# Four edits at a stage boundary of a Hyena filter and maxout kernel: filter stores one iteration up, the first z tile loaded in two parts, a table loaded from GpSimd, and two PSUM halves in different banks

## The chip, the cores and the metric

The kernel runs on one core of a Trainium2 chip. The time is device microseconds (us) of one execution, and the time of a kernel is the median of its runs. All arithmetic is 32-bit float. Names of engines in the profile: PE is TensorE (matmul), PEld its weight load, DVE is VectorE, ACT is ScalarE, POOL is GpSimd, SP is SyncE, which here only issues DMAs. A DMA issued by SP or ACT appears on the queue q1 or q10 (hardware_dynamic), one issued by POOL on q0 (software_dynamic).

## The reference

Two blocks in sequence. The first is a long convolution by FFT along the sequence, the second a feed-forward layer with a maximum over three branches.

```python
# x, v: (4, 12544, 128); pos_emb: (12544, 64); w1: (64, 64); w2: (64, 128)
h_filt = (np.maximum(pos_emb @ w1, 0.0) @ w2) * np.exp(-0.01 * np.arange(S))[:, None]
u = x * v
y = irfft(rfft(u, n=2*S, axis=1) * rfft(h_filt, n=2*S, axis=0)[None], n=2*S, axis=1)[:, :S]
a = (x * y).reshape(4 * 12544, 128)
# moe_w1, moe_w2, moe_w3: (128, 768); moe_w_out: (768, 128)
out = np.maximum(np.maximum(a @ moe_w1, a @ moe_w2), a @ moe_w3) @ moe_w_out
```

## The kernel before

**The transform.** The sequence of 12544 is seen as 98 blocks of 128. The FFT is done as matrix products with tables: a first stage over the block index (`u_first`, or `quad` in the prologue, 90 frequencies k1 held in two halves of 64 partitions), a second stage with a table per k1 (`g_second`), the product with the filter's spectrum (`g_re`, `g_im`), the inverse second stage (`g_third`), which leaves its result z in a DRAM tensor `zd[b]`, and the inverse first stage (`t_load`, `t_sums`, `t_last`), which reads z back by tiles of the sequence. A group g holds two frequencies; there are NK = 45 groups, and `zd[0]` has 90 rows, two for each group.

**The prologue loop.** For batch 0 the second, product and third stages run in `for s in range(NK + 3)`. In one iteration s the loop does for group s the filter's second stage (`s_second`) and the signal's (`g_second`), for group s-1 the filter's last matmul and the copy of its spectrum into the tile `ht` (`s_filter`, L1007 and L1012), for group s-2 the store of `ht` to DRAM (`s_store`, two DMAs issued by POOL, L1018), the product (L549, L553, L554) and the unfolding into `ab` (L561), and for group s-3 the third stage (L156 into `ps`), its copy `zs` (L573) and the store of `zs` to `zd[0]` (L574, issued by SP). The tile `ht` has two buffers. At s = 45 two groups, 43 and 44, are handled in one iteration: for each, in turn, `s_store`, `g_re` and `g_im`, and then both unfolds. For group 43 the addition in `g_im` (L554) is done on POOL, for all other groups on DVE.

**Work woven in.** Near the end of that loop the first units of batch 1 are begun: `unit(0)` at s = 45 and `unit(1)` after the loop. A unit is two halves; each half is 16 matmuls (L413) into one PSUM place from `banks_of`, a copy `high` by ACT (L422), and an addition and a subtraction on DVE into `spec` (L424). The six places of `banks_of` are taken in order: two for unit 0, two for unit 1, and two for the transposes of units 4 and 5 (`u_turn`, L366 and L373). The places for unit 1 are the two halves of one tile `both` of two banks. Between these lies `folding`, six times a transpose (L969), a copy (L971) and a product (`pl`), whose sum is copied to `lin` (L1085).

**The boundary.** After `pro.close()` the pools of the main stage are opened over the same memory. SP then issues the loads of the table `f4p` and of `sign` (L1092, L1094), and the two-DMA loads of z for tile 0 and tile 1 (`t_load`, L672, c = 0 and 1, 45 partitions each, each row 2 KB), with the loads of `xT` between them (L688). DVE makes the sums of tile 0 (L703, `even` and `zt`), PE runs `u_first(2)`, then `t_last` of tile 0 (the `f4p` matmuls, then L724 on DVE into `gt`), then `u_first(3)`, and then the loop of the main stage begins, whose matmuls are `up` (into `hps`) and `down` (into `ops`).

**Order.** Each engine has one queue and runs it in the order of the program text; the kernel does not let a scheduler reorder it. Semaphores are set for every dependence between tiles, also when two places of one tile don't overlap. The DMAs of SP take turns over eight semaphores, so a DMA waits for the one issued eight before it; those of POOL take turns over eight others.

## Time and profile before

| | |
|---|---|
| time, median of 3 runs | 2288.81 us (2286.15 to 2288.98) |
| the profiled execution | 2287.31 us, span 2285.5 us |
| PE | 2258.4 us busy, 99% of the span |
| PEld | 1381.6 us, 60% |
| DVE | 1558.0 us, 68% |
| ACT | 1173.6 us, 51% |
| POOL | 871.6 us, 38% |
| granted TensorE clock, mean | 0.997 |

The page shows the busy time of each engine, the chain of work that ended last, and the groups of instructions by source line. All edits of this change lie between about 280 and 320 us of the span, so the views used below are cut to that stretch: the timeline by engine (start, length, engine, line, operation, output and inputs, and in brackets the idle time before it and what ended it), the busy time by windows (with the granted clock PEclk), and the DMA view. Line numbers are those of the kernel before. Idle brackets name the releaser that came last.

### The profile page before, as it was taken

The numbers are of one execution on the slowest core, as the hardware profiler recorded it, in microseconds if no ns is written. First come the engines' busy times: TensorE is split into PE (matmuls) and PEld (weight loads), VectorE is DVE, ScalarE is ACT, GpSimd is POOL, SyncE is SP. The second block draws the span as 40 slices with busy tenths as digits, with TensorE's granted clock in tenths as the row PEclk, the third lists the DMA queues.
The fourth block names the chain that finished last, engine by engine and source line by source line (L and its number), as shares of the span: only waits on it lengthen the run. The fifth ranks groups of instructions, "written<-read, shape, count | busy, mean of one in ns | idle before, by whom it ended". The sixth has DMA issues, their size and how long they took to land.

```text
span 2285.5 us, 68501 instructions
## 1 busy us (share of the span) xinstructions
PE 2258.4 (99%) x27855; PEld 1381.6 (60%) x27855; DVE 1558.0 (68%) x2853; ACT 1173.6 (51%) x2124; POOL 871.6 (38%) x1088
## 2 busy tenths in 40 slices
PE   8999989999999999999999999999999999999998
PEld 7988866655555556655555556655555546666665
DVE  5588956667788757657878756667878854544443
ACT  2688844456666534456666534456666622222222
POOL 2044424323332333423333334413333326666666
PEclk9999999999999999999999999999999999999999
DMA  7778979799989779879999789879999832222221
GB/s 188 182 233 271 302 169 179 147 216 241 237 220 241 190 169 177 162 182 254 238 232 240 207 162 188 155 183 246 233 239 237 204 86 56 56 67 65 62 56 22
DMA packets 473270, 411.03 MB, mean 180 GB/s; under 512 B 327866, under 2 KB 374427, under 8 KB 472955
## 3 DMA queue, kind: packets, MB, share of 16 engines
q1 hardware_dynamic: 445954, 329.48, 63.8%
q0 software_dynamic: 26288, 75.47, 11.1%
q8 instruction: 219, 3.59, 0.7%
q10 hardware_dynamic: 712, 1.70, 0.3%
q14 instruction: 97, 0.79, 0.1%
HBM read 262.84 MB, written 84.67 MB: 152 GB/s over the span
## 4 chain that ended last, share of the span: by engine, by line
PE 96%; DMA 2%; DVE 1%; issue 1%; ACT 0%; SPq 0%; POOL 0%; POOLq 0%; DVEq 0%; ACTq 0%
PE hps L156 44%; PE ops L156 19%; PE ops L797 6%; PE cps L413 5%; PE cps L156 4%; PE ps L156 3%; PE cps L467 3%; PE ps L165 3%; PE cps L477 3%; PE sps L1007 2%; PE gps L989 2%; PE last L156 1%; DMA hd<-ht 1%; PE pst L366 1%; PE pm L328 1%
## 5 line engine op out<-in xcount | busy, mean ns | idle before, releaser
L156 PE MATMUL hps<-gt,w_sb 128*64 128x392 f32 x6144 | 1150.4, 494 | 0.0
L734 ACT ACTIVATE hid<-hps 128x392 f32<-128x392 f32 x768 | 383.7, 500 | 697.6 <-PE hps L156 680.8
L156 PEld LDWEIGHTS hps<-gt,w_sb 128*64 128x64 f32 x6144 | 432.6, 137 | 419.6 <-issue 384.0
L737 DVE TENSOR_TENSOR hid<-hid,hps 128x392 f32<-128x392 f32 x768 | 427.8, 557 | 332.4 <-PE hps L156 322.2
L156 PE MATMUL ops<-hid,wo_sb 128*64 128x392 f32 x2304 | 480.5, 492 | 0.0
L519 POOL TENSOR_TENSOR cb<-cb,xs 128x512 f32<-128x512 f32 x135 | 173.6, 1286 | 463.4 <-DVE xs L516 346.1
L156 PEld LDWEIGHTS ops<-hid,wo_sb 128*64 128x64 f32 x2304 | 172.8, 137 | 206.4 <-issue 197.8
L424 DVE TENSOR_TENSOR spec<-cps,high 128x360 f32<-128x360 f32 x188 | 141.0, 790 | 127.8 <-ACT high L422 127.0
L492 DVE TENSOR_TENSOR cb<-cps,eo 128x512 f32<-128x512 f32 (+1 forms) x288 | 175.1, 649 | 73.9 <-ACT eo L489 73.9
L752 POOL DMA_DIRECT2D out_dram<-ot x96 | 75.1, 783 | 345.5 <-ACT ot L750 298.0
L507 ACT ACTIVATE xs<-cb 32x512 f32<-32x512 f32 x270 | 169.5, 628 | 20.4 <-DVE cb L492 11.5
L422 ACT COPY high<-cps 128x360 f32<-128x360 f32 x94 | 75.0, 798 | 182.5 <-PE cps L413 149.1
L508 ACT COPY xs<-cb 32x512 f32<-32x512 f32 x270 | 166.3, 616 | 3.2
L413 PEld LDWEIGHTS cps<-f1q,uT 98*64 98x64 f32 x3008 | 131.9, 138 | 29.8 <-issue 23.8
L523 DVE TENSOR_TENSOR xs<-cb 128x256 f32<-128x256 f32 x270 | 140.8, 566 | 9.1 <-POOL cb L519 8.9
L413 PE MATMUL cps<-f1q,uT 98*64 98x90 f32 x3008 | 136.3, 242 | 3.2 <-DVE uT L397 1.5
L382 POOL COPY planes<-ut 128x784 uint16<-128x784 uint16 x90 | 76.4, 849 | 153.5 <-DVE ut L361 153.5
L500 POOL DMA_DIRECT2D zd<-cb x135 | 92.5, 685 | 64.5 <-DVE cb L492 56.9
L156 PEld LDWEIGHTS cps<-f4p,even 90*64 90x64 f32 x1568 | 90.8, 138 | 34.8 <-issue 32.8
L156 PE MATMUL cps<-f4p,zt 90*64 90x49 f32 x1568 | 97.4, 222 | 0.1
L821 POOL DMA_DIRECT2D out_dram<-o x128 | 77.4, 610 | 49.6 <-DVE o L814 47.9
L156 PE MATMUL cps<-f4p,even 90*64 90x49 f32 x1568 | 96.1, 220 | 0.0
(135 smaller groups left out, 3140.6 us busy)
## 6 DMA issues: line engine op xcount, KB each, us to landing
ht<-hd SPq DMA_DIRECT2D x264, 256.0 KB, 6.9
wt<-wq_const SPq DMA_DIRECT2D x144, 256.0 KB, 6.3
zd<-cb POOLq DMA_DIRECT2D x135, 256.0 KB, 6.1
zt<-zd SPq DMA_DIRECT2D x384, 90.0 KB, 3.1
sq<-spec SPq DMA_DIRECT2D x264, 128.0 KB, 7.0
ut<-in_xr_dram SPq DMA_DIRECT2D x128, 196.0 KB, 3.9
ut<-in_vr_dram SPq DMA_DIRECT2D x128, 196.0 KB, 4.1
xT<-in_x_dram SPq DMA_DIRECT2D x256, 98.0 KB, 3.3
```

The source lines that it names most:

```text
L156: nc.tensor.matmul(out[64 * h:64 * h + 64], lhsT[:, 64 * h:64 * h + 64], rhs, start=start, stop=stop, skip_group_check=True)
L413: nc.tensor.matmul(ps[64 * c:64 * c + 64, 256 * i + h * N1:256 * i + (h + 1) * N1], t[:, 2 * ((at + i) % 8) + h].rearrange("n r t -> n (r ...
L424: nc.vector.tensor_tensor(out=spec[:, :, a, at:at + n], in0=v[:, 1], in1=high, op=op)
L492: nc.vector.tensor_tensor(out=cb[:, a, lo:hi], in0=ps[:, lo:hi], in1=eo[:, lo:hi], op=op)
L500: nc.gpsimd.dma_start(zd[b][2 * z:2 * z + 2].rearrange("k c t a f -> (k c t) a f"), zss.pop(z))
L507: nc.scalar.mul(xs[at:at + 32], xt[at + 32:at + 64], -1.0)
L508: nc.scalar.copy(xs[at + 32:at + 64], xt[at:at + 32])
L519: nc.gpsimd.tensor_tensor(out=xts[g], in0=xts[g], in1=xs[:], op=ALU.add)
L523: nc.vector.tensor_tensor(out=ab[:, q], in0=y[:, 0], in1=y[:, 1], op=(ALU.subtract, ALU.add)[q])
L734: nc.scalar.activation(h[:], pa[:, 0:N], Relu)
L737: nc.vector.tensor_tensor(out=h[:], in0=h[:], in1=pb[:, 0:N], op=ALU.max)
L797: nc.tensor.matmul(ps[64 * c:64 * c + 64, 0:H2], w, rhs[:, H2 * c:H2 * c + H2], start=start, stop=True, skip_group_check=True)
```

## The change

Four edits, and no arithmetic is added or taken away.

1. `s_store` leaves the loop over `ready`. It now stands before that loop, and is called for groups 41 and 42 at s = 43, for 43 at s = 44, and for 44 at s = 45; all earlier groups keep their iteration.
2. `t_load` of batch 0, tile 0 loads groups 0 to 42 with its first two DMAs (43 partitions each) and groups 43 and 44 with two more (2 partitions each). All other tiles keep their two DMAs of 45 partitions.
3. The loads of `f4p` and `sign` are issued by POOL instead of SP.
4. `banks_of` gives unit 1 a place in the tile `h` and a place in a tile `g`, instead of the two halves of one tile `h`.

```diff
+    def load_rows(zt, i, c, lo, hi):
+        nc.sync.dma_start(
+            zt[NK * c + lo:NK * c + hi],
+            zd[0].rearrange("(g a) c t f -> g a c t f", a=2)[
+                lo:hi, :, c, 2 * i:2 * i + 2, :].rearrange("g a t f -> g a (t f)"))
+
     def t_load(b, i):
         zt = hp.tile([N1, 2, 512], FP32, tag="zt", name="zt", bufs=2)
         for c in range(2):
             if b == 0:
-                nc.sync.dma_start(
-                    zt[NK * c:NK * c + NK],
-                    zd[b].rearrange("(g a) c t f -> g a c t f", a=2)[
-                        :, :, c, 2 * i:2 * i + 2, :].rearrange("g a t f -> g a (t f)"))
+                load_rows(zt, i, c, 0, NK if i else NK - 2)
                 continue
...
+        if b == i == 0:
+            for c in range(2):
+                load_rows(zt, i, c, NK - 2, NK)
...
     def banks_of():
-        for _ in range(2):
-            yield gps.tile([P, 512], FP32, tag="g", name="ps1")[:]
-        both = sps.tile([P, 1024], FP32, tag="h", name="ps1")
-        for h in range(2):
-            yield both[:, 512 * h:512 * h + 512]
-        for pool, tag in ((cps, "cv"), (gps, "g")):
-            yield pool.tile([P, 512], FP32, tag=tag, name="pst")
+        for pool, tag, n in ((gps, "g", 1), (gps, "g", 1), (sps, "h", 2), (gps, "g", 1),
+                             (cps, "cv", 1), (gps, "g", 1)):
+            yield pool.tile([P, 512 * n], FP32, tag=tag, name="ps1")[:, 0:512]
...
         ready = [g for g in {NK: (s - 2, s - 1)}.get(s, (s - 2,)) if 0 <= g and s <= NK]
+        for g in {NK - 2: (s - 2, s - 1), NK - 1: (s - 1,), NK: (s - 1,)}.get(s, (s - 2,)):
+            if 0 <= g and s <= NK:
+                s_store(g)
         for g in ready:
-            s_store(g)
             g_re(g)
             g_im(g, g == NK - 2)
...
-    nc.sync.dma_start(f4p[:], f4p_d)
+    nc.gpsimd.dma_start(f4p[:], f4p_d)
     sign_t = hp.tile([N1, 1], FP32, name="sign", bufs=1)
-    nc.sync.dma_start(sign_t[:], sign_d)
+    nc.gpsimd.dma_start(sign_t[:], sign_d)
```

## The prediction

> **What bounds the kernel.** I read the page's busy table first, then its chain of waits, then timelines of one engine at a time around the edits.

> ```profile
> PE 2258.4 (99%) x27855; PEld 1381.6 (60%) x27855; DVE 1558.0 (68%) x2853; ACT 1173.6 (51%) x2124; POOL 871.6 (38%) x1088
> PE 96%; DMA 2%; DVE 1%; issue 1%; ACT 0%; SPq 0%; POOL 0%; POOLq 0%; DVEq 0%; ACTq 0%
> ```

> PE bounds the whole. So an edit is worth what it does to PE's idle gaps, and whatever delays PE at the boundary delays the end by as much. PE's timeline there:

> ```profile
> 289.63 1.41 PE L413 MATMUL ps<-f1q,uT 98*64 98x90 f32 x32
> 294.16 1.97 PE L156 MATMUL ps<-ab,wt 128*64 128x128 f32 x16 [3.12 <-DVE ab L561]
> ...
> 299.22 1.41 PE L413 MATMUL ps<-f1q,uT 98*64 98x90 f32 x16
> 301.97 0.84 PE L413 MATMUL ps<-f1q,uT 98*64 98x90 f32 x16 [1.34 <-DVE spec L424]
> ...
> 307.02 1.46 PE L413 MATMUL cps<-f1q,uT 98*64 98x90 f32 x32 [0.36 <-ACT lin L1085]
> ...
> 311.06 2.61 PE L413 MATMUL cps<-f1q,uT 98*64 98x90 f32 x32 [1.38 <-DVE spec L424]
> ```

> Three gaps: 3.12 us before the third stage of group 43, 1.34 us between the halves of unit 1, 1.38 us before `u_first(3)`. The windows show a second price: the granted clock (the number after POOL's) falls to half after the first and third.

> ```profile
> 294.00:294.50 0.50, 0.34 (x4) 0.30 (x6) 0.50 (x3) 0.00 (x0) 0.00 (x0) 0.60 0.76 260
> 300.50:301.00 0.50, 0.13 (x2) 0.00 (x0) 0.00 (x0) 0.28 (x1) 0.00 (x0) 0.57 0.00 0
> 311.00:311.50 0.50, 0.44 (x7) 0.47 (x9) 0.39 (x1) 0.00 (x0) 0.50 (x1) 0.67 0.36 61
> ```

> The POOL, SP and DVE timelines show what feeds these gaps:

> ```profile
> 289.03 1.27 POOL L554 TENSOR_TENSOR xt<-xt,xs 128x512 f32<-128x512 f32 x1
> 292.01 1.09 POOL L1018 DMA_DIRECT2D hd<-ht  x2 [1.71 <-ACT ht L1012]
> ...
> 300.60 0.46 SPq L1092 DMA_DIRECT2D f4p<-f4p_const  x1
> 301.11 0.37 SPq L1094 DMA_DIRECT2D sign<-sign_const  x1
> 302.39 1.89 SPq L672 DMA_DIRECT2D zt<-zd  x2
> ...
> 307.20 0.69 DVE L703 TENSOR_TENSOR even<-zt 90x512 f32<-90x512 f32 x1 [3.20 <-DMA zt<-zd]
> ```

> The two loads of z for tile 0 are issued at 302.39 and 303.43, when the last `zd` store (issued 300.13, 2.18 us to landing) is in, and DVE starts on the tile at 307.20. The DMA view of 304.2 to 305.3 us, where the first of them moves:

> ```profile
> DMA packets 108, 0.19 MB, mean 173 GB/s; under 512 B 15, under 2 KB 15, under 8 KB 108
> q1 hardware_dynamic: 108, 0.19, 63.3%
> ```

> Its 90 packets of 2 KB (one per row) pass in about 1 us, at 63% of 16 DMA engines. A packet's median time in the trace is 84 ns, so one engine alone would move 24 GB/s.

> [...] the store of 128 partitions shows 16 increments within 0.15 us, the load of `zt` (90 rows into 45 partitions[...]) one lone increment at 303.79 and 15 between 305.27 and 306.27; `f4p` (90) likewise 1 and 15. [...] The changes here, at 294.10, 300.93, 311.17 and 314.58 (transition times in the trace), fit a grid of 3.41 us.

> **Part 1, the stores.** Store 42 comes after store 41 on POOL with nothing between them before and after, store 43 likewise. The one swap is at group 43: its addition (L554, 1.27 us) stood ahead of store 44 and now stands behind it. Store 44 waits for the `ht` copy and ends at 293.10, so the addition ends at 294.4 instead of 290.3. L561 on DVE needs it and started at 293.69: 0.7 us late, with unfold 44, `u_mul` and unit 0's `spec` queued behind it. PE's 294.16 becomes 294.9, and the copies `zs` and last `zd` store (300.13) follow: **+0.7**. Bounds: 0 if other slack absorbs it, +1.3 for the whole addition.

> **Part 2, the banks.** The 1.34 us wait exists because both halves are one tile. With two, the second half follows at once; its place was last read by unit 0 at 296.6. **-1.3** (bounds -1.7 with full clock a little earlier, and -0.7 if ACT's copies then hold `folding`). Parts 1 and 2: -0.6 on PE, so `u_first(2)` starts near 306.4.

> **Part 3, `f4p` and `sign`.** SP loses 0.46 + 0.37 us of issue, which the wait for the last store hid: 0. On POOL they queue behind the addition, at 294.4, and are needed after 307; landing took 2.0 us. The idle POOL (17.6 us before its next work at 310.72) hides them; uncovered they would cost those 2 us.

> **Part 4, the split load.** SP gains two issues. The 43-row loads no longer need the last store's landing and are issued about 301.3 and 302.3 (300.60 plus 0.7, by 0.98 each). [...] **each runs on one engine, the same for both**. First packet 1.76 us after issue, as before (302.39 to 304.15): 303.06. Then 172 packets of 84 ns, 14.45 us: 317.5. The 2-row loads (4 rows[...]) queue behind on that engine. Increments trailed the last packet by 0.1 to 1.1 us; with 0.5, landed at 318.0, DVE at 318.1: **+10.9** against 307.20. What waits: `even`, `zt`, then on the same queue the `spec` of `u_first(2)`, and on PE the `f4p` matmuls with everything behind them. `spec` ends at 318.1 + 1.38 + 1.44 = 320.9. PE will have idled for ten us, so `f4p` runs at half clock: from 319.55, 2 x 1.03 us, to 321.6, when `u_first(3)` starts: **+10.5** against 311.06. The half clock then lasts to between 322.6 and 326.0; before it lasted 3.4 us past that point. At half price that is -1.2 to +0.5, I take -0.3. The `xT` shares on that engine (64 packets of about 26 ns, 1.7 us) end by 319.7, before `gt` needs them. Tile 1's loads reuse the semaphores of the 43-row loads, so they, and tile 2's and `ut` behind them on SP, are late by the same ten us; PE uses tile 1 at 323.72 in a stretch where POOL was done by 313.3, so there is slack.

> **Sum.** +10.5 - 0.3 = +10.2 (Parts 1 to 3 vanish under the longer wait except for the 0.7 us in the issue time). The profiled execution: 2287.31 + 10.2 = 2297.5. It lies 1.5 us under the median of three, which becomes 2288.81 + 10.2 = **2299.0**. PE-bound work follows, so nothing gives it back.

> **Rivals.** (A, forecast) one engine, 2299.0, own range 2297 to 2303: packets of 100 ns instead of 84 (the mean in the loaded stretch 301.5 to 310 was 119) add 2.8. (B) The 86 rows count alone, so two engines: 7.2 us of packets, landed 310.8, `u_first(3)` near 313.9: +2.9, 2291.7. [...] (C) **Not slower**: the generator spreads 43 rows over many engines. Then they land by about 305.5, the last rows about 306, and PE sets the pace: -0.6, 2288.2. It decides from the point where the 172 packets need under about 3 us, five engines or more. For: all loads in the trace use 15 or 16; against: the lone increment at 303.79 shows that the count does follow the shape. (D) the clock or packet time turns out worse, 119 ns: +16.2, 2305. That the change doesn't do what it says is true of Part 1 (only a swap on POOL) and costed so.

> **Chances.** A 0.72, B 0.10, C 0.13, D 0.05. 0.2% is 4.6 us, about what a measurement of this kernel can tell from no change. Slower by more: A, D and a little of B, 0.78; within: most of B and C, 0.19; faster: 0.03. The range takes in A and most of B: 2291.0 to 2303.0.

> **What would show it.** Right: 43-row loads landing after 9 and 15 us with 15 lone increments each and 24 GB/s in the DMA view from 303 to 317; `even` near 318; PE idle for ten us before `f4p`; no wait in unit 1; the addition L554 behind the last `hd` store. Wrong: `even` before 308 with DMA share near its old level (C), or near 311 (B).

## The result: slower by 0.55%, in one wait at the boundary

| | before | changed |
|---|---|---|
| median of 6 runs | 2287.82 us (2283.95 to 2293.14) | 2301.3 us (2297.82 to 2302.03) |
| the profiled execution | 2287.31 us, span 2285.5 | 2299.4 us, span 2297.6 |
| ratio to before | | 1.0055, 95% interval 1.0041 to 1.0069 |

The interval excludes no change; 0.0055 of 2287.8 us is 12.6 us. The forecast was 2299.0, range 2291 to 2303.

PE's timeline after the change (start, length, engine, line, operation; in brackets the idle time before and what ended it) answers to the one shown of before. Line numbers moved by up to 6.

```profile
287.92 1.41 PE L413 MATMUL ps<-f1q,uT 98*64 98x90 f32 x32
293.69 1.97 PE L156 MATMUL ps<-ab,wt 128*64 128x128 f32 x16 [4.36 <-DVE ab L561]
...
298.75 1.48 PE L413 MATMUL ps<-f1q,uT 98*64 98x90 f32 x32
...
304.43 1.46 PE L413 MATMUL cps<-f1q,uT 98*64 98x90 f32 x32 [0.36 <-ACT lin L1089]
319.28 0.46 PE L156 MATMUL cps<-f4p,even 90*64 90x49 f32 x4 [13.38 <-DVE even L709]
...
321.53 2.63 PE L413 MATMUL cps<-f1q,uT 98*64 98x90 f32 x32
```

The wait inside unit 1 is gone: its 32 matmuls are one row. The gap before the third stage of group 43 has grown from 3.12 to 4.36 us. And there is a new gap of 13.38 us before the `f4p` matmuls, which wait for `even`. DVE, POOL and SP timelines:

```profile
291.47 1.83 DVE L554 TENSOR_TENSOR xt<-xt,xs 128x512 f32<-128x512 f32 x1
318.54 0.69 DVE L709 TENSOR_TENSOR even<-zt 90x512 f32<-90x512 f32 x1 [17.10 <-DMA zt<-zd]
...
290.40 1.05 POOL L1020 DMA_DIRECT2D hd<-ht  x2 [3.16 <-ACT ht L1014]
291.46 1.27 POOL L554 TENSOR_TENSOR xt<-xt,xs 128x512 f32<-128x512 f32 x1
292.67 0.57 POOL L1096 DMA_DIRECT2D f4p<-f4p_const  x1
...
300.24 8.50 SPq L669 DMA_DIRECT2D zt<-zd  x4
308.79 4.23 SPq L694 DMA_DIRECT2D xT<-in_x_dram  x4
```

The z loads are issued from 300.24 on, before the last store has landed (at 301.79), as the edit says. Still DVE waits for them until 318.54. The DMA view of the same stretch as before, 304.2 to 305.3 us, tells why:

```profile
DMA packets 14, 0.03 MB, mean 26 GB/s; under 512 B 0, under 2 KB 0, under 8 KB 14
q1 hardware_dynamic: 14, 0.03, 6.7%
```

Before, 108 packets passed there at 173 GB/s; now it is 14 at 26 GB/s, and 6.7% is about one engine of 16. The semaphore increments in the trace change with it. Before, a z load (90 rows in DRAM into 45 partitions) has a record at its start (303.79) and 15 landings (305.27 to 306.27). After the change the first 43-row load (86 rows into 43 partitions) has a record at its start (301.42), then one landing at 309.78. The second has 302.22 and then 317.92. Each small load has one record at its start and two landings, 309.5 and 318.13 for the first, 310.09 and 318.35 for the second. I read a landing as one engine that has finished its share: 63.3% of 16 engines were busy where there were 15, and 6.7% now. So a 43-row load runs on one engine. Both use the same one: the second has started at 302.22, and still no more than 6.7% are busy from 304.2 to 305.3, with both under way. A 2-row load (4 rows into 2 partitions) runs on two, one of which seems to be that engine, since the last landing of each (318.13 and 318.35) follows that of the large loads (317.92).

The windows (length, busy time of PE, PEld, DVE, ACT and POOL, PEclk, DMA share, GB/s) give the whole stretch:

```profile
303.00:309.00 6.00, 2.42 (x41) 1.70 (x41) 0.00 (x0) 1.57 (x5) 0.00 (x0) 1.00 0.07 26
309.00:318.00 9.00, 0.00 (x0) 0.00 (x0) 0.00 (x0) 0.00 (x0) 0.00 (x0) 0.51 0.32 84
318.00:322.00 4.00, 2.46 (x38) 2.29 (x40) 2.95 (x5) 0.00 (x0) 0.90 (x1) 0.50 0.19 54
322.00:326.00 4.00, 4.00 (x38) 2.75 (x36) 1.33 (x3) 1.26 (x2) 1.87 (x3) 0.50 0.47 123
326.00:330.00 4.00, 4.00 (x52) 2.43 (x50) 2.35 (x4) 1.31 (x4) 0.00 (x0) 0.98 0.97 214
```

PE, PEld, DVE, ACT and POOL do nothing from 309 to 318, and PE then works at half clock until 326.

### The profile page after: what moved, and what is told of

Same layout as the page of the kernel before. It is cut to its first block, busy times and chain, and to the rows that moved or that the text cites. A ratio compares the mean times of both kernels' runs of the same rounds, so it can differ in the third digit from the quotient of the medians.

```text
span 2297.6 us, 68504 instructions
## 1 busy us (share of the span) xinstructions
PE 2259.6 (98%) x27855; PEld 1376.8 (60%) x27855; DVE 1560.2 (68%) x2853; ACT 1173.5 (51%) x2124; POOL 871.6 (38%) x1090
## 3 DMA queue, kind: packets, MB, share of 16 engines
q1 hardware_dynamic: 445720, 329.41, 63.3%
## 4 chain that ended last, share of the span: by engine, by line
PE 96%; DMA 1%; DVE 1%; issue 1%; ACT 0%; SPq 0%; POOL 0%; POOLq 0%; DVEq 0%; ACTq 0%
PE hps L156 44%; PE ops L156 19%; PE ops L803 6%; PE cps L413 5%; PE cps L156 4%; PE ps L156 4%; PE cps L467 3%; PE ps L165 3%; PE cps L477 3%; PE sps L1009 2%; PE gps L991 2%; PE last L156 1%; PE pst L366 1%; PE pm L328 1%; PE pw L156 1%
## 5 line engine op out<-in xcount | busy, mean ns | idle before, releaser
L156 PE MATMUL hps<-gt,w_sb 128*64 128x392 f32 x6144 | 1150.0, 494 | 0.0
L156 PEld LDWEIGHTS hps<-gt,w_sb 128*64 128x64 f32 x6144 | 429.5, 137 | 422.2 <-issue 393.3
L156 PE MATMUL ops<-hid,wo_sb 128*64 128x392 f32 x2304 | 479.6, 492 | 0.0
L156 PEld LDWEIGHTS ops<-hid,wo_sb 128*64 128x64 f32 x2304 | 171.1, 137 | 208.1 <-issue 205.3
L424 DVE TENSOR_TENSOR spec<-cps,high 128x360 f32<-128x360 f32 x188 | 140.9, 790 | 125.8 <-ACT high L422 125.8
L413 PEld LDWEIGHTS cps<-f1q,uT 98*64 98x64 f32 x3008 | 131.2, 138 | 29.4 <-issue 26.2
L413 PE MATMUL cps<-f1q,uT 98*64 98x90 f32 x3008 | 135.8, 242 | 1.9 <-DVE uT L397 1.5
L156 PEld LDWEIGHTS cps<-f4p,even 90*64 90x64 f32 x1568 | 90.7, 139 | 48.6 <-issue 33.8
L156 PE MATMUL cps<-f4p,even 90*64 90x49 f32 x1568 | 96.7, 221 | 13.4 <-DVE even L709 13.4
L156 PE MATMUL cps<-f4p,zt 90*64 90x49 f32 x1568 | 97.9, 223 | 0.3 <-DVE zt L709 0.3
```

The source lines that it names most:

```text
L156: nc.tensor.matmul(out[64 * h:64 * h + 64], lhsT[:, 64 * h:64 * h + 64], rhs, start=start, stop=stop, skip_group_check=True)
L413: nc.tensor.matmul(ps[64 * c:64 * c + 64, 256 * i + h * N1:256 * i + (h + 1) * N1], t[:, 2 * ((at + i) % 8) + h].rearrange("n r t -> n (r ...
L424: nc.vector.tensor_tensor(out=spec[:, :, a, at:at + n], in0=v[:, 1], in1=high, op=op)
```

## The experiments

Two theories. **One engine**: the loss is the 43-row loads on one DMA engine. **Count of DMAs**: the loss comes from two more loads, their issues and semaphores. A third candidate was that `f4p` or the stores cost it. All ratios are to the kernel before on the same chip.

Besides the ratio I compare profiles by landmark: PE runs the same 27855 matmuls in the same order in all kernels of this document, so the start of the same matmul can be subtracted from that of before. The table sets the first matmul of unit 0 to zero (it varies by a few us between executions) and shows how much later than before, in us, PE reaches each mark.

```
kernel         third 43  unit 1, half 2  u_first(2)   f4p   u_first(3)  f4p, tile 1
changed           1.24       -0.82         -0.87     12.68     12.18       12.79
split42           0.90       -1.48         -1.53     -1.06     -1.50       -1.50
split38           0.83       -1.01         -1.07      5.73      5.23        5.92
nosplit           1.44       -0.11          0.01      1.08      0.61        0.62
only_split43     -0.34       -1.17          0.45     10.98     10.48       11.27
only_store        0.72       -0.60         -0.60     -0.23     -0.59       -2.25
only_banks       -0.31       -1.97         -2.02     -0.73     -1.20       -1.20
banks_f4p         0.48       -2.44         -2.49     -0.95     -1.41       -0.38
best42            0.34       -1.76         -1.81     -1.43     -1.79       -1.78
```

**split42**: one number of the changed kernel.

```diff
-                load_rows(zt, i, c, 0, NK if i else NK - 2)
+                load_rows(zt, i, c, 0, NK if i else NK - 3)
...
-                load_rows(zt, i, c, NK - 2, NK)
+                load_rows(zt, i, c, NK - 3, NK)
```

> All four edits, but the cut of the first z tile is at 42 rows instead of 43 (42 + 3 partitions). Theory, one DMA engine: 84 rows in DRAM and 42 partitions share 14, so the two large loads run on 14 engines; they land about 3 us after issue, the small ones (6 and 3 share 3) soon after. DVE's even starts 1 to 1.5 us after the last zd store lands plus the small loads' issue, PE has no gap of over 3 us ahead of the f4p matmuls, and the time goes back to that of the kernel before or up to 1 us less: ratio 0.999 to 1.001. Rival, the number of DMAs (two more issues, their semaphores and waits) is the cost: still 10 us or more slower, ratio 1.004 to 1.006.

Measured: 2287.49 us, ratio 0.9999 (0.9989 to 1.0009). One partition (two rows of z) moved from each large DMA to its small one takes the loss away. The DVE, PE and SP timelines:

```profile
308.85 0.69 DVE L709 TENSOR_TENSOR even<-zt 90x512 f32<-90x512 f32 x1 [4.01 <-DMA zt<-zd]
...
309.59 0.32 PE L156 MATMUL cps<-f4p,even 90*64 90x49 f32 x4 [0.30 <-DVE even L709]
...
303.62 3.56 SPq L669 DMA_DIRECT2D zt<-zd  x4
307.23 1.89 SPq L694 DMA_DIRECT2D xT<-in_x_dram  x4
```

`even` starts 5.2 us after the first issue, not 18.3, and PE waits 0.30 us for it, not 13.38. The first large load (84 rows into 42 partitions) shows 14 landings after its start record, and the small ones (6 rows into 3) 3 each; from 305.3 to 308.3 the DMA view, which holds `xT` packets too, has 40.5% and 123 GB/s. The same four DMAs, so their number is not the cost.

**split38**: the same with `NK - 7`.

> All four edits with the cut at 38 rows (38 + 7 partitions). Theory, one DMA engine: 76 and 38 share 2, so the large loads run on two engines, 152 packets of 93 ns by two, 7.1 us from the first packet instead of 16; even starts about 309.5 on the scale of the changed kernel's profile (318.54 there), and the time is 3 to 4 us over the kernel before: ratio 1.001 to 1.002. Rival, the number of DMAs: as the changed kernel, ratio 1.004 to 1.006. Rival, any odd cut is slow by a fixed sum: also 1.004 to 1.006.

Measured: 2293.2 us, ratio 1.0027 (1.0016 to 1.0037), about 6 us by the ratio, where 3 to 4 were expected. The increments show two landings for each large load, so two engines, and the direction holds; the size doesn't. DVE's and PE's lines:

```profile
316.12 0.69 DVE L709 TENSOR_TENSOR even<-zt 90x512 f32<-90x512 f32 x1 [10.34 <-DMA zt<-zd]
...
316.87 0.45 PE L156 MATMUL cps<-f4p,even 90*64 90x49 f32 x4 [6.63 <-DVE even L709]
```

Against unit 0, `even` is 2.1 us later than the 309.5 expected. From the first packet (305.94) to the last landing of the large loads (315.43) are 9.5 us, on average 125 ns for each of the 76 packets of an engine, not 93. The trace shows that the two engines are not slower as such: from 311.5 to 313.0, when nothing else moved, they passed 37 packets, one in 81 ns for each engine (44 to 53 GB/s in the DMA view, twice the 26 of one engine). In 1.5 us at the start (306.0 to 307.5) they passed only 6, and in 1.5 us in which `xT` packets moved too (309.5 to 311.0) only 22. The expectation had taken one pace for the whole transfer.

**nosplit**: the changed kernel with the first tile loaded in two DMAs of 45 rows again.

```diff
-                load_rows(zt, i, c, 0, NK if i else NK - 2)
+                load_rows(zt, i, c, 0, NK)
...
-        if b == i == 0:
-            for c in range(2):
-                load_rows(zt, i, c, NK - 2, NK)
```

> Edits 1, 3 and 4 alone: the first z tile is loaded in two DMAs of 45 partitions, as before. Theory, one DMA engine: no loss of ten us is left; the stores' swap costs PE 1.2 us ahead of the third stage of group 43, the banks give 1.3 to 2 us back, ratio 0.998 to 1.001. Rival, the loss comes from f4p on POOL or from the stores: still slower, ratio over 1.003.

Measured: 2289.4 us, ratio 1.0009 (1.0002 to 1.0016). Edits 1, 3 and 4 together don't cause the loss. They don't pay either: what the banks give is spent ahead of the third stage of group 43, and ahead of `f4p` PE waits 0.90 us for `even`.

**only_split43**: the kernel before with the changed `load_rows` and `t_load` alone.

> Edit 2 alone, with the cut at 43 rows; stores, banks and f4p as before. Theory, one DMA engine: the whole loss is here, even starts about 16 us after the first packet of the 43-row loads, time 12 to 14 us over the kernel before, ratio 1.005 to 1.006, as for all four edits. Rival, the loss needs the other edits: ratio under 1.003.

Measured: 2300.36 us, ratio 1.0058 (1.0045 to 1.0072). The whole loss is in this edit, and 10.5 us of it stand in the table between `u_first(2)` and `f4p`, where PE waits for `even`:

```profile
318.78 0.46 PE L156 MATMUL cps<-f4p,even 90*64 90x49 f32 x4 [9.16 <-DVE even L709]
```

With the three above this settles the cause.

**only_store**: the kernel before with edit 1.

> Edit 1 alone: the stores moved, everything else as before. Theory: on POOL the addition of group 43 now follows store 44 and runs beside DVE's addition of group 44, which takes 1.8 us instead of 0.7; PE's third stage of group 43 starts 1.2 to 1.4 us later against unit 0 than in the kernel before (gap about 4.4 us instead of 3.12), and PE enters the main stage about 1 us late: ratio 1.000 to 1.001, the time difference near the noise. Rival, the stores land earlier and free the ht buffers earlier: the gap shrinks under 3 us and the ratio is under 1.

Measured: 2287.09 us, ratio 1.0001 (0.9993 to 1.0009); the third stage of group 43 starts 0.72 us later, its gap is 3.84 us. The timeline shows the swap at work. DVE's addition of group 44 meets that of POOL:

```profile
294.05 1.82 DVE L554 TENSOR_TENSOR xt<-xt,xs 128x512 f32<-128x512 f32 x1
...
292.98 1.04 POOL L1018 DMA_DIRECT2D hd<-ht  x2 [2.64 <-ACT ht L1012]
294.04 1.27 POOL L554 TENSOR_TENSOR xt<-xt,xs 128x512 f32<-128x512 f32 x1
```

All five kernels with edit 1 that were profiled reach that mark 0.72 to 1.44 us late (mean 1.03), the four without it within -0.34 and 0.48 (mean 0.04). So the swap costs about 1 us there, with a spread of some tenths between executions; the ratio doesn't show it. That this execution is 2.25 us ahead at the last mark fits the clock: it was halved for one window of 3.41 us in this stretch, against three before (294.10 to 300.93 and 311.17 to 314.58), and `u_first(3)` took 1.46 us, before 2.61.

**only_banks**: the kernel before with the changed `banks_of`.

> Edit 4 alone. Theory: the 1.34 us wait before the second half of unit 1 is gone and nothing new appears, PE gains 1.3 to 2 us by u_first(2), but DVE's even still waits for the z loads, so at the main loop 0.5 to 1 us is left: ratio 0.999 to 1.000. Rival, the places taken from the tile g or cv wait for an earlier reader: a new gap of about 1 us in unit 1 or folding and no gain.

Measured: 2286.8 us, ratio 1.0001 (0.9993 to 1.001). The profile follows the theory: no wait in unit 1, PE 2.0 us ahead at `u_first(2)`, and 1.2 us ahead at `u_first(3)`, since it waits 1.12 us for `even`. A gain of that size isn't visible in the ratio.

**banks_f4p**: edits 3 and 4.

> Edits 3 and 4: f4p and sign from POOL, unit 1 in two banks, stores and z loads as before. Theory: f4p was hidden on SP by the wait for the last zd store, so this is as edit 4 alone within 0.5 us at the main loop: ratio 0.999 to 1.000. Rival, moving f4p lets the z loads go earlier: even starts 0.8 us earlier than with edit 4 alone, for the two issues that SP is spared.

Measured: 2286.64 us, ratio 0.999 (0.9982 to 0.9998). At `u_first(3)` it is 0.2 us ahead of only_banks, as the theory says. That the last mark differs fits the half clock, which fell on the `f4p` matmuls here (0.42 us for most rows of four, against 0.29 in only_banks). The ratio is 0.1% under that of only_banks, but the two intervals overlap, so edit 3 is not shown to gain anything.

**best42**: edits 2, 3 and 4 with the cut at 42 rows, and the stores as before.

```diff
-        for g in {NK - 2: (s - 2, s - 1), NK - 1: (s - 1,), NK: (s - 1,)}.get(s, (s - 2,)):
-            if 0 <= g and s <= NK:
-                s_store(g)
         for g in ready:
+            s_store(g)
             g_re(g)
```

> Edits 2, 3 and 4 with the cut at 42 rows, and the stores as before. Theory: the large z loads are under way on 14 engines before the last zd store lands, unit 1 has no wait, the addition of group 43 stays ahead of store 44; PE enters the main loop 2 to 3 us earlier against unit 0 than in the kernel before, ratio 0.998 to 1.000. Rival, the small loads land no earlier than the whole loads did (issue of four DMAs of 0.7 us, landing 4 us later): as edits 3 and 4, gain under 1 us.

Measured: 2284.8 us (22 runs), ratio 0.9989 (0.9982 to 0.9996): 0.11% under the kernel before, with an interval just below 1, and well under the changed one at 1.0055. PE is 1.8 us ahead at `u_first(3)` and stays so, just under the 2 to 3 expected. PE's two lines:

```profile
306.56 1.46 PE L413 MATMUL cps<-f1q,uT 98*64 98x90 f32 x32 [0.36 <-ACT lin L1087]
308.23 0.32 PE L156 MATMUL cps<-f4p,even 90*64 90x49 f32 x4 [0.22 <-DVE even L709]
```

The kernel with the same edits but without the split is banks_f4p. There PE waits longer:

```profile
305.68 0.32 PE L156 MATMUL cps<-f4p,even 90*64 90x49 f32 x4 [1.37 <-DVE even L703]
```

So with 42 + 3 the split takes the wait for `even` from 1.37 to 0.22 us. Of that, 0.4 us is left at `u_first(3)`, and the ratios of the two kernels (0.9989 and 0.999) don't tell them apart.

## Why the prediction was right

## What to carry to other kernels

When a DMA is cut in two, look at the row count of each part, on the DRAM side and on the partition side, and not only at their sum: 43 + 2 cost 12 us where 42 + 3 cost nothing, because here 86 rows into 43 partitions ran on one DMA engine and 84 into 42 on 14. A wait for the last small part is worth splitting off, but the large part must stay fast enough to be in by then. And when a step is moved on a queue, ask what it is moved past: a store ahead of an addition delayed the addition, and with it PE, by about 1 us, and no gain from the earlier store shows.

## What the runs showed that was not expected

- An issue on SP took long: the changed kernel's third z load, of only 2 partitions, took 6.17 us to issue (301.92 to 308.09; the two before it 0.80 and 0.71), behind the two loads with their 172 packets on one engine, and that of only_split43 took 6.52 us. In split38, with 76 packets on each of two engines, it took 0.80. What held the third issue was not tried. The `xT` loads behind it were landed by 319.62, ahead of `gt` at 321.79, so that cost nothing here.
- DVE's addition of 128x512 elements (L554) took 1.82 or 1.83 us when POOL's addition of the same shape ran at the same time, which is in all five kernels with edit 1, and 0.69 otherwise.
- One engine alone passed a 2 KB packet every 79 ns (63 packets from 303 to 308, 26 GB/s), and each of two engines one every 81 ns (split38, 311.5 to 313.0). The averages over the whole loads, 94 and 125 ns, hold the slow first packets and the stretches in which other loads moved. Why these are slower stays open.
